# Two neighbouring attention groups in one run of score matmuls and one run of value matmuls

## The chip, the cores and the metric

The kernel runs on one core of a Trainium2 chip. The metric is the device time of one execution in microseconds (us); the median of three runs of the kernel before is 906.98 us (906.97 to 907.12). A core has a matrix engine (TensorE, PE in the profile, with its weight loads listed as PEld), a vector engine (DVE), a scalar engine (ACT) and a sync engine (SP) that issues the DMA transfers. Matmuls write into PSUM, which has eight banks of 2 KB in each of its 128 partitions; DVE and ACT read the banks.

## The reference

Three stages follow each other. Sparse attention over 4 batches, 8 heads, 576 positions and head width 64: in heads 0 to 3 a position looks back over the last 32 positions, in heads 4 to 7 over the earlier positions with the same remainder modulo 32. Then a two-layer MLP, then a gated MLP, both on 2304 tokens of width 512:

```
scores = q @ k^T / 8, masked;  attn = softmax(scores);  x = attn @ v        # 2304 x 512
x = leaky_relu(x @ moe_w_in, 0.01) @ moe_w_out                              # 512 -> 2048 -> 512
out = (sigmoid(x @ moe2_w_gate) * (x @ moe2_w_val)) @ moe2_w_out            # 512 -> 1536 -> 512
```

The weights arrive as 64-bit numbers; the kernel turns their bits into 32-bit words and splits each value into a high and a low part, so that each product is done as three fp32r matmuls (high by high, high by low, low by high; lines 329 to 331).

## The kernel before, in words

**Attention groups.** The 576 positions of each batch are halved: eight chunks `c` of 288 positions. A group is one chunk and one pair of heads (`pr`). Pairs 0 and 1 are local heads: five blocks of 64 queries by 96 keys. Pairs 2 and 3 are strided heads: five blocks of 63 queries by 63 keys in an even chunk; in an odd chunk the keys are 126, and the five blocks make two groups of three and two. That gives 40 groups in the order of `CORDER`, even chunks first. The first four groups have their own buffers.

**A group's work** (class `Group`): loads of q, k and v (lines 475 to 494); scores (line 509, tile `sc`, two matmuls a block, one for each head of 64 rows); masks by DVE (line 529, into `e`), row maxima (line 535), exponentials with their sums by ACT (line 540), the reciprocals and the scaling on DVE (lines 547 to 555); transposes of `e` on TensorE (line 564, tile `pt`), copied by ACT into `pts` (line 570); values (line 581, tile `xo`); and two parts of the result written as a high part by ACT (line 600) and a low part by DVE (line 598) into `x`. Scores use the four 64 by 64 quarters of the TensorE array, values its two column halves (or the quarters where there are 63 keys); transposes and MLP matmuls use the whole array.

**First MLP.** Class `First` takes one chunk of tokens and one slice of 128 hidden units: 12 matmuls from `x` into `h` (lines 329 to 331), ACT twice over `h` (lines 703 and 706), DVE once (line 710), and 12 matmuls from `gh`, `gl` into `y`. A run of 12 such matmuls of 256 columns is called an MLP run below. A token chunk can start when its groups have written `x`, so MLP runs of earlier chunks are laid between the attention work of later ones. Class `Job` prepares weights on ACT and DVE (lines 133 to 182).

**What sets the order.** All operations up to the end of the first MLP go into one list planner (class `Plan`). An operation has an engine, a cost in ns, operations that it comes after, a rank and rooms that it takes and gives. `Plan.order` places the operations by these costs, and the instructions of each engine then stand in that order and are executed in it. Rooms are buffers: `sc` is one pair of PSUM banks for scores (mm0, mm1; the `h` tiles use mm2 and mm3 during attention), `ax` two banks for transposes and values, `pts` two buffers, `e` and `st` three, `qk` three, `v` two. SP issues all loads from one queue in the planned order, so a load that waits for its buffer holds up the loads behind it.

**How banks are guarded.** In the built program an instruction waits for the last one that touched the tile it needs: a mask waits until the matmuls into its `sc` bank are done.

Of the kernel before, what the change touches and what calls it, by code (L numbers as in the profile page):

```python
# [7 lines left out]
F32 = mybir.dt.float32  # L8
# [8 lines left out]
P = 128  # L17
# [12 lines left out]
NB = 5  # L30
# [33 lines left out]
SPLIT = 2  # L64
OPS = 12
T0 = 256
GATES, OPERAND_PAIRS, LAG = 6, 8, 2

CONST_W = P + 2 * LW + SW[0] + SW[1]
# [3 lines left out]
def attention_mlp_glu(ctx: ExitStack, tc: tile.TileContext, qT, kl, ks0, ks1, vl, vs0, vs1, w1, w2, wg, wv, w3, const, out):  # L73
# [19 lines left out]
    def bank(tag, shape, name):  # L93
        return ps.tile(shape, F32, tag=tag, bufs=1, name=name)
# [191 lines left out]
    for c in range(NC2):  # L286
        quarter = {n: parts_tile(("p", c, n), [P, 2, 512]) for n in range(1, 8)}
        for m, w in enumerate((wg, wv)):
            d = {n: quarter[n][:, m, :] for n in quarter}
            a, b = Job((w, 2 * c)), Job((w, 2 * c + 1))  # L290
            a.whole = b.whole = False
            a.dest, b.dest, b.only = [d[1], d[2]], [None, d[3]], 1
            t = Sums(a, b, None, [d[5], d[6]])
# [15 lines left out]
    for i in range(len(cells) + 1):  # L309
        mine = [(i, "p", n) for n in ORDER] if i < len(cells) else []  # L310
# [24 lines left out]
    ap = att_pool.__enter__()  # L335
# [107 lines left out]
    class Group:  # L443


        def __init__(self, c, pr, blocks):
            self.c, self.pr, self.blocks, self.nb = c, pr, blocks, len(blocks)
            self.b, self.half = divmod(c, 2)
            self.local = pr < 2
            if self.local:  # L450
                self.w = LW
                self.q0 = [LOC[i] for i in blocks]
                self.k0 = [max(0, self.half * TA + LOC[i] - STRIDE) for i in blocks]
                self.nq = [LOC_N[i] for i in blocks]
                self.skip = [64 - n for n in self.nq]
            else:
                self.w = SW[self.half]
                self.q0 = [RES[i] * HP for i in blocks]
                self.k0 = [RES[i] * HP * (self.half + 1) for i in blocks]
                self.nq = [RES_N[i] * HP for i in blocks]  # L460
                self.skip = [SQ - n for n in self.nq]

            self.cut = (self.nb + 1) // 2

        def side(self, n, h):

            h = h if n < self.cut else 1 - h
            return slice(64 * h, 64 * h + 64)

        def buffers(self):  # L470
# [22 lines left out]
            src = vl[b, pr, self.half] if self.local else (vs0, vs1)[self.half][b, pr - 2]  # L493
            nc.sync.dma_start(out=self.v[:w, :nb, :], in_=src[:, self.blocks[0] : self.blocks[0] + nb, :])

        def scores(self, at):
            nb, w, cut = self.nb, self.w, self.cut
            sc = [
                bank(f"mm{j + 2 * ('h' in at)}", [P, z - a, w], f"sc{a}") for j, (a, z) in enumerate(((0, cut), (cut, nb)))
            ]  # L500
            for i in range(cut):
                for n in (i, cut + i):
                    if n >= (cut, nb)[n >= cut]:
                        continue
                    q0, k0 = self.q0[n] - self.q0[0], self.k0[n] - self.k0[0]
                    for h in range(2):
                        r = slice(64 * h, 64 * h + 64)
                        o = self.side(n, h)
                        nc.tensor.matmul(
                            sc[n >= cut][o, n - cut * (n >= cut), :], self.q[r, q0 : q0 + 64], self.k[r, k0 : k0 + w],  # L510
                            start=True, stop=True,
                        )
            self.sc = sc

        def parts(self):
            if self.local and self.half == 0:
# [42 lines left out]
        def tr(self, a, z, at):  # L559
            if a == 0:  # L560
                self.pt = {}
            self.pt[a] = bank(f"ax{at['ax'][0]}", [P, z - a, P], "pt")
            for n in range(a, z):
                nc.tensor.transpose(self.pt[a][: self.w, n - a, :], self.e[:, n, :], ident)

        def pts(self, a, z, at):
            w = self.w
            if a == 0:
                self.p = ap.tile([P, NB, P], F32, tag=f"pt{at['pts'][0]}", bufs=1, name="pts")
            nc.scalar.copy(self.p[:w, a:z, :], self.pt[a][:w, :, :])  # L570

        def pv(self, at):
# [26 lines left out]
            else:  # L599
                nc.scalar.copy(dst[0], src)  # L600

        def plan(self, n):

            nb, w, total = self.nb, self.w, sum(self.nq)
            rank = (1, n)
            self.buffers()
            qk, v = [] if self.c == 0 else ["qk"], [] if self.c == 0 else ["v"]
            me = self
            self.sc_room = ["h", "h"] if self.c == 0 and n % 2 else ["sc"]
            ax = ("ya", "yb")[n % 2] if self.c == 0 else "ax"  # L610
            lq = plan.add("SP", 4 * P * (self.q0[-1] + 64 - self.q0[0]), self.load_q, rank=(LOAD(n, 0),), me=me, take=qk)
            lk = plan.add(
                "SP", 4 * P * (self.k0[-1] + w - self.k0[0]), self.load_k, rank=(LOAD(n, 0) + 0.01,), me=me, then=[lq]
            )
            lv = plan.add("SP", 4 * w * nb * P, self.load_v, rank=(LOAD(n, 1),), me=me, take=v)
            sc = plan.add(
                "PE", 100 * nb, self.scores, rank=rank, me=me, kind="sc", after=[lq, lk], take=self.sc_room,
                give=qk,
            )
            before, parts = [sc, plan.const[0 if self.local else 2]], self.parts()  # L620
            for j, (a, z, _) in enumerate(parts):
                op = plan.add(
                    "DVE", (z - a) * w / 0.96 + 67, lambda at, j=j: self.mask(j, at), rank=(1, n, 0), me=me, after=before,
                    take=["e", "st"] if j == 0 else [], give=self.sc_room if j == len(parts) - 1 else [],
                )
                before = [op]
            op = plan.add("DVE", nb * w / 0.96 + 67, self.top, rank=(1, n, 1), me=me, after=before)
            op = plan.add("ACT", nb * (180 + w / 1.2 + 100 - 10), self.exps, rank=rank, me=me, after=[op])
            self.key = op
            op = plan.add("DVE", 75, self.eps, rank=(1, n, 2), me=me, after=[op])  # L630
            op = plan.add("DVE", 95, self.inverse, rank=(1, n, 3), me=me, after=[op])
            op = plan.add("DVE", nb * w / 0.96 + 67, self.norm, rank=(1, n, 4), me=me, after=[op], give=["st"])
            copies = []
            for a in range(0, nb, 3):
                z = min(a + 3, nb)
                t = plan.add(
                    "PE", 109 * (z - a), lambda at, a=a, z=z: self.tr(a, z, at), rank=rank, me=me, kind="pt", after=[op, plan.const[1]],
                    take=["ax"], give=["e"] if z == nb else [],
                )
                copies.append(  # L640
                    plan.add(
                        "ACT", (z - a) * P / 1.2 + 57, lambda at, a=a, z=z: self.pts(a, z, at), rank=rank, me=me, after=[t],
                        take=["pts"] if a == 0 else [], give=[("ax", t)],
                    )
                )
            pv = plan.add(
                "PE", 1.0 * total * 1.85, self.pv, rank=rank, me=me, kind="xo", after=copies + [lv], take=[ax],
                give=["pts"] + v,
            )
            self.done = []  # L650
            for s0, s1 in ((0, HP - 1), (HP - 1, HP)):
                m = total * (s1 - s0) // HP
                op = plan.add(
                    "ACT", m / 1.2 + 57, lambda at, s0=s0, s1=s1: self.put(s0, s1, False, at), rank=rank, me=me, after=[pv]
                )
                op = plan.add(
                    "DVE", m / 0.96 + 67, lambda at, s0=s0, s1=s1: self.put(s0, s1, True, at), rank=(1, n, 5), me=me,
                    after=[op], give=[(ax, pv)] if s0 else [],
                )
                self.done.append(op)  # L660

    groups = []
    for c in CORDER:
# [193 lines left out]
    total, last_read = {}, {}  # L857
# [275 lines left out]
    def load_const(a, z):  # L1133
        nc.sync.dma_start(out=cst[:, a:z], in_=const[:, a:z])

    plan = Plan(
        {
            "place": RING, "qk": 3, "v": 2, "e": 3, "st": 3, "sc": 1, "h": 2, "ax": 2, "ya": 1, "yb": 1, "pts": 2, "early": EARLY, "late": EARLY, "raw": STAGED, "w32": WORDS, "split": 1, "late split": SPLIT, "sums": 2,
        }
    )  # L1140
    unit_done, unit_place = {}, {}
    for j, (a, z) in enumerate(consts):
        op = plan.add("SP", 4 * P * (z - a), lambda at, a=a, z=z: load_const(a, z), rank=((0.5, 1.5, 2.5)[j],), me=plan)
        plan.const.append(op)
    for n, g in enumerate(groups):
        g.plan(n)

    def to_late(at):
        att_pool.__exit__(None, None, None)
# [14 lines left out]
    for j in range(RING, RING + n_a):  # L1164
        op = plan.add(
            "SP", 4096 * P, lambda at, j=j: fetch(j), rank=(-2000 + j,), after=[jobs[ready[uses[j]]].kept], then=before,
            take=["place"], me=plan,
# [14 lines left out]
    after = [op for item in final if item.t0 < 2 * TP for op in item.flushed]  # L1182
    after += [item.entered for item in final if item.t0 < XCUT] + [plan.add("-", 0, to_small, rank=(0,), me=plan, after=[item.left for item in items[:REGION]])]
    for n, name in enumerate(MAKE):
        steps = operand_steps(0, name)
        for engine, cost in enumerate((867, 735, 867)):
            if engine or name[0] == "s":
                op = plan.add(
                    ("DVE", "ACT", "DVE")[engine], cost, lambda at, steps=steps, engine=engine: steps(engine), rank=(1, n), me=plan,
                    after=after,  # L1190
# [122 lines left out]
```

## Time and profile before

| what | value |
|---|---|
| median of 3 runs | 906.98 us |
| the profiled execution, its own time | 909.16 us |
| its span, first to last instruction | 907.4 us |
| TensorE busy | 886.8 us (98%) |
| DVE busy | 714.3 us (79%) |
| ACT busy | 455.6 us (50%) |
| DMA | 214.49 MB, mean 236 GB/s |
| chain that ended last | TensorE 82% of the span |

The profiled execution took 1.8 us more than its span, for what lies before the first and behind the last instruction, and 2.2 us more than the median. Attention begins at once and its last value matmuls are done at 167.4 us; from then on TensorE has only whole-array matmuls. In the timeline each row is one instruction or several equal ones merged; an fp32 matmul of scores or values shows up as two rows' worth (x20 for the ten matmuls of a five-block group).

### The profile page before, as it was taken

Reading aid. Unit: us, or ns where it says so; the run is one execution under the profiler, and the core shown is the slowest. Engines: PE = TensorE matmul, PEld = TensorE weight load, DVE = VectorE, ACT = ScalarE, POOL = GpSimd, SP = SyncE. Lnnn points to the kernel's source line nnn. Section 1 sums busy time; section 2 is a strip of 40 time slices with the busy share of each in tenths; the row PEclk is TensorE's granted clock in tenths of the full one; section 3 lists DMA queues with packets and bytes.
Section 4 is the critical chain, followed back from the end, with each engine's and each line's share of the span. In section 5 each row is a group of like instructions: output and inputs, shape, how many; then the busy total and the mean of one; then the engine's idle time right before and its main releaser. Section 6 shows DMA issues by size and latency. Waiting matters only on the chain.

```text
span 907.4 us, 17636 instructions
## 1 busy us (share of the span) xinstructions
PE 886.8 (98%) x6399; PEld 831.5 (92%) x6399; DVE 714.3 (79%) x1570; ACT 455.6 (50%) x1196; POOL 0.2 (0%) x4
## 2 busy tenths in 40 slices
PE   6899999999999999999999999999999999999997
PEld 5788788998888999888899999999999999999997
DVE  6798899856888877787796767779967778667775
ACT  6688888544444444443553653335453344443331
POOL 0000000000000000000000000000000000000000
PEclk9889999999999999999999999999999999999999
DMA  8444846657676689664639877777887777887762
GB/s 247 146 149 128 264 123 213 215 224 295 233 264 222 215 285 408 221 244 164 216 137 321 319 240 251 256 251 258 257 311 254 252 246 266 293 280 246 243 233 70
DMA packets 81686, 214.49 MB, mean 236 GB/s; under 512 B 10216, under 2 KB 21832, under 8 KB 81600
## 3 DMA queue, kind: packets, MB, share of 16 engines
q1 hardware_dynamic: 81600, 213.37, 69.6%
q8 instruction: 51, 0.84, 0.4%
q14 instruction: 35, 0.29, 0.1%
HBM read 164.84 MB, written 48.50 MB: 235 GB/s over the span
## 4 chain that ended last, share of the span: by engine, by line
PE 82%; DMA 6%; DVE 5%; ACT 3%; issue 1%; SPq 1%; ACTq 0%; DVEq 0%
PE h L329 6%; PE h L330 6%; PE h L331 6%; PE y L329 5%; PE y L330 5%; PE y L331 5%; PE g L879 5%; PE g L880 5%; PE v L881 5%; PE v L880 5%; PE v L879 5%; PE g L881 5%; PE o L935 5%; PE o L934 5%; PE o L933 5%; DMA raw<-w 3%
## 5 line engine op out<-in xcount | busy, mean ns | idle before, releaser
L948 DVE TENSOR_TENSOR sum_o<-o,sum_o 128x512 f32<-128x512 f32 x214 | 110.4, 549 | 34.9 <-PE o L935 34.8
L329 PE MATMUL h<-x,u 128*128 128x256 f32 (+2 forms) x384 | 132.6, 345 | 0.0
L329 PE MATMUL y<-gh,u 128*128 128x256 f32 (+2 forms) x384 | 131.3, 342 | 0.6 <-ACT sum_y L738 0.5
L330 PE MATMUL h<-x,u 128*128 128x256 f32 (+2 forms) x384 | 130.3, 339 | 0.0
L331 PE MATMUL h<-x,u 128*128 128x256 f32 (+2 forms) x384 | 130.2, 339 | 0.0
L330 PE MATMUL y<-gl,u 128*128 128x256 f32 (+2 forms) x384 | 129.4, 337 | 0.1
L331 PE MATMUL y<-gh,u 128*128 128x256 f32 (+2 forms) x384 | 129.3, 337 | 0.0
L935 PE MATMUL o<-u,gl 128*128 128x256 f32 x357 | 100.6, 282 | 0.0
L934 PE MATMUL o<-u,gh 128*128 128x256 f32 x357 | 100.4, 281 | 0.0
L933 PE MATMUL o<-u,gh 128*128 128x256 f32 x357 | 100.1, 280 | 0.0
L914 ACT CAST gh<-gate 128x384 fp32r<-128x384 f32 x123 | 63.2, 514 | 70.2 <-DVE gate L904 42.4
L879 PE MATMUL g<-ops,u 128*128 128x384 f32 x252 | 84.8, 336 | 0.0
L880 PE MATMUL g<-ops,u 128*128 128x384 f32 x252 | 84.5, 335 | 0.0
L881 PE MATMUL g<-ops,u 128*128 128x384 f32 x252 | 84.4, 335 | 0.0
L879 PE MATMUL v<-ops,u 128*128 128x384 f32 x252 | 84.2, 334 | 0.0
L880 PE MATMUL v<-ops,u 128*128 128x384 f32 x252 | 84.2, 334 | 0.0
L881 PE MATMUL v<-ops,u 128*128 128x384 f32 x252 | 84.2, 334 | 0.0
L329 PEld LDWEIGHTS h<-x,u 128*128 128x128 f32 x384 | 74.0, 193 | 8.0 <-issue 1.9
L703 ACT ACTIVATE gh<-h 128x256 fp32r<-128x256 f32 (+2 forms) x96 | 46.8, 488 | 67.3 <-PE y L331 61.0
L329 PEld LDWEIGHTS y<-gh,u 128*128 128x128 f32 x384 | 72.9, 190 | 7.5 <-issue 0.9
L330 PEld LDWEIGHTS h<-x,u 128*128 128x128 f32 x384 | 74.1, 193 | 5.7
L331 PEld LDWEIGHTS h<-x,u 128*128 128x128 f32 x384 | 74.0, 193 | 5.6
(83 smaller groups left out, 1908.5 us busy)
## 6 DMA issues: line engine op xcount, KB each, us to landing
u<-parts SPq DMA_DIRECT2D x203, 512.0 KB
parts<-split SPq DMA_DIRECT2D x127, 256.0 KB
raw<-w SPq DMA_DIRECT2D x44, 512.0 KB
parts<-split SPq DMA_DIRECT2D x20, 512.0 KB
raw<-wg SPq DMA_DIRECT2D x12, 512.0 KB
raw<-wv SPq DMA_DIRECT2D x12, 512.0 KB
out<-sum_o SPq DMA_DIRECT2D x16, 256.0 KB
u<-parts SPq DMA_DIRECT2D x15, 256.0 KB
```

Source lines behind the costliest of these rows:

```text
L329: nc.tensor.matmul(o, wu[:, 0, a:b], xh, start=start, stop=False)
L330: nc.tensor.matmul(o, wu[:, 0, a:b], xl, start=False, stop=False)
L331: nc.tensor.matmul(o, wu[:, 1, a:b], xh, start=False, stop=stop)
L703: nc.scalar.activation(out=self.g[0], in_=self.h, func=AF.Prelu, alpha=SLOPE)
L879: nc.tensor.matmul(o, wh, xh, start=first and k == 0, stop=False, **more)
L880: nc.tensor.matmul(o, wh, xl, start=False, stop=False, **more)
L881: nc.tensor.matmul(o, wl, xh, start=False, stop=k == 1, **more)
L914: nc.scalar.copy(self.part[name][0], self.tile[0, n])
L933: nc.tensor.matmul(o, gh, u[:, 0:256], start=first and r % 2 == 0, stop=False, **more)
L934: nc.tensor.matmul(o, gh, u[:, 256:512], start=False, stop=False, **more)
L935: nc.tensor.matmul(o, gl, u[:, 0:256], start=False, stop=True, **more)
L948: nc.vector.tensor_tensor(out=acc, in0=o, in1=acc, op=ALU.add)
```

## The change

From the fifth group on, groups are planned two at a time: 18 pairs of neighbours, which always have the same chunk and the same key width. `pair_scores` lays the scores of both into the same two banks, the second group's halves crosswise (`turned`), and issues both groups' matmuls one after the other; both groups' masks must be done before the banks are free again. `pair_pv` issues the values of both groups in one run; it takes both `ax` banks. A group's two sets of transposes now follow each other on TensorE (`then=self.turns`), and the `pts` buffer is taken by the transposes, not by the copy behind them. A pair's two `v` buffers come free together behind the pair's values, and its two `qk` buffers behind the pair's scores. The order of all engines changes, since the planner places everything anew.

```diff
+PAIRED = 4
...
+            self.cut, self.turned = (self.nb + 1) // 2, False
...
+            h = h if (n < self.cut) != self.turned else 1 - h
...
+        def pair_scores(self, other, at):
+
+            a, b, c, d = self.cut, self.nb - self.cut, other.nb - other.cut, other.cut
+            both = [bank(f"mm{j}", [P, n, self.w], f"sc{j}") for j, n in enumerate((a + c, b + d))]
+            self.sc = [both[0][:, :a, :], both[1][:, :b, :]]
+            other.sc = [both[1][:, b:, :], both[0][:, a:, :]]
+            other.turned = True
+            for g in (self, other):
+                g.scores(at, both)
+
+        def pair_pv(self, other, at):
+            for n, g in enumerate((self, other)):
+                g.pv({"ax": at["ax"][n:]})
...
                 t = plan.add(
                     "PE", 109 * (z - a), lambda at, a=a, z=z: self.tr(a, z, at), rank=rank, me=me, kind="pt", after=[op, plan.const[1]],
-                    take=["ax"], give=["e"] if z == nb else [],
+                    then=self.turns, take=["ax"] + (["pts"] if a == 0 else []),
+                    give=["e"] if z == nb else [],
                 )
+                self.turns = [t]
...
+    def plan_groups(n, mine):
+
+        for i, g in enumerate(mine):
+            g.plan_loads(n + i)
+        first, single = mine[0], len(mine) == 1
+        sc_room = ["h", "h"] if first.c == 0 and n % 2 else ["sc"]
+        ax = ("ya", "yb")[n % 2] if first.c == 0 else "ax"
+        sc = plan.add(
+            "PE", sum(100 * g.nb for g in mine), first.scores if single else lambda at: first.pair_scores(mine[1], at),
+            rank=(1, n), me=first, kind="sc", after=[op for g in mine for op in g.loads[:2]], take=sc_room,
+        )
+        for g in mine:
+            plan.free([sc], g, *g.held[0])
+            g.plan_softmax(sc)
+        plan.free([g.masked for g in mine], first, *sc_room)
+        pv = plan.add(
+            "PE", sum(1.85 * sum(g.nq) for g in mine), first.pv if single else lambda at: first.pair_pv(mine[1], at),
+            rank=(1, n), me=first, kind="xo", after=[op for g in mine for op in g.copies + g.loads[2:]], take=[ax] * len(mine),
+        )
...
-    for n, g in enumerate(groups):
-        g.plan(n)
+    n = 0
+    while n < len(groups):
+        mine = groups[n : n + (2 if n >= PAIRED else 1)]
+        plan_groups(n, mine)
+        n += len(mine)
```

TensorE in the steady part, before: the scores of the 15th group (`sc_1124`, line 509) and the values of the 11th (line 581), between transposes (`pt`) and MLP runs (`h`, `y`).

```order
L331 MATMUL h<-x_61,u_996 128x256
L564 MATMUL pt<-cst,e 63x128 x2
L564 MATMUL pt<-cst,e 96x128 x3
L509 MATMUL sc_1124<-k,q 64x63 x2
L509 MATMUL sc_1125<-k,q 64x63 x2
...
L581 MATMUL xo<-pts,v 64x63 x8
L581 MATMUL xo<-pts,v 64x36 x2
L564 MATMUL pt<-cst,e 96x128 x2
L329 MATMUL y<-gh,u_632 128x256
```

TensorE at the corresponding place in the changed kernel: the scores of the 13th and 14th group in the banks `sc_899` and `sc_900` (line 513), directly followed by the values of the 9th and 10th group (line 597).

```order
L332 MATMUL h<-x_61,u_358 128x256
L582 MATMUL pt<-cst,e 96x128 x5
L513 MATMUL sc_899<-k,q 64x96 x2
L513 MATMUL sc_900<-k,q 64x96 x2
...
L597 MATMUL xo<-pts,v 64x64 x8
L597 MATMUL xo<-pts,v 64x32 x2
...
L330 MATMUL h<-x_61,u_425 128x256
```

In the first, one group's scores and one group's values stand between transposes that use the whole array, and a group's transposes stand in two pieces; in the second, two groups' scores and two groups' values follow each other, and the five transposes of a group are together.

ACT behind the first MLP runs, before: `gh` and `g` are the two passes over `h`, line 540 the exponentials of the fifth and then the sixth group, line 177 a step of the weights.

```order
L703 ACTIVATE gh<-h 128x256
L706 ACTIVATE g<-h 128x256
L540 ACTIVATE e,st<-e,st 128x96 x5
L703 ACTIVATE gh<-h 128x256
L177 CAST u_518<-w 128x512
L706 ACTIVATE g<-h 128x256
L540 ACTIVATE e,st<-e,st 128x96 x5
```

ACT at the same place in the changed kernel (line 557 the exponentials, 745 and 748 the passes over `h`).

```order
L745 ACTIVATE gh<-h 128x256
L748 ACTIVATE g<-h 128x256
L178 CAST u_474<-w 128x512
L745 ACTIVATE gh<-h 128x256
L748 ACTIVATE g<-h 128x256
L557 ACTIVATE e,st<-e,st 128x96 x10
```

The exponentials of the fifth group have moved behind the passes over the second `h`, and those of the sixth follow at once.

## Rows read from the trace of the kernel before

**Rows 1.** Busy time by stretch: bounds, length, each engine's busy us, clock, DMA, GB/s.

```profile
20.00:54.24 34.24, 29.02 (x357) 24.74 (x355) 28.52 (x88) 25.49 (x108) 0.00 (x0) 0.82 0.59 177
54.24:167.42 113.18, 110.63 (x1476) 97.84 (x1475) 101.99 (x330) 93.62 (x390) 0.00 (x0) 1.00 0.56 174
110.00:140.00 30.00, 29.91 (x400) 26.24 (x400) 29.47 (x100) 25.16 (x105) 0.00 (x0) 1.00 0.51 156
167.42:907.40 739.98, 734.55 (x4423) 699.50 (x4419) 571.60 (x1118) 323.24 (x643) 0.00 (x0) 1.00 0.72 248
```

**Rows 2.** Timeline of TensorE around 110 us: start, duration, line, tiles, count.

```profile
109.02 0.28 PE L331 MATMUL h<-x,u 128*128 128x256 f32 x1
109.23 0.78 PE L581 MATMUL xo<-pts,v 96*64 96x64 f32 x20
109.93 0.53 PE L564 MATMUL pt<-cst,e 128*96 128x128 f32 x3
110.39 0.65 PE L509 MATMUL sc<-k,q 64*64 64x126 f32 x12
110.97 0.39 PE L329 MATMUL y<-gh,u 128*128 128x256 f32 x1
111.19 0.28 PE L330 MATMUL y<-gl,u 128*128 128x256 f32 x1
111.31 0.28 PE L331 MATMUL y<-gh,u 128*128 128x256 f32 x1
...
112.51 0.71 PE L564 MATMUL pt<-cst,e 128*96 128x128 f32 x5
112.97 0.36 PE L329 MATMUL h<-x,u 128*128 128x256 f32 x1
```

**Rows 3.** The same view, where two groups' values already follow each other.

```profile
114.58 1.15 PE L581 MATMUL xo<-pts,v 96*64 96x64 f32 x32
115.66 0.45 PE L509 MATMUL sc<-k,q 64*64 64x126 f32 x8
```

**Rows 4.** Timeline of TensorE: the first MLP run, and the first of the second chunk.

```profile
22.10 1.20 PE L509 MATMUL sc<-k,q 64*64 64x96 f32 x18
23.23 0.58 PE L329 MATMUL h<-x,u 128*128 128x256 f32 x1
...
51.53 0.56 PE L329 MATMUL h<-x,u 128*128 128x256 f32 x1
...
52.53 0.41 PE L330 MATMUL h<-x,u 128*128 128x256 f32 x1
52.75 0.41 PE L331 MATMUL h<-x,u 128*128 128x256 f32 x1
```

**Rows 5.** What TensorE waited for, 54.24 to 167.42: us, times, longest.

```profile
PE xo L581 <- DMA v<-vs: 1.6, 2, 0.9
```

**Rows 6.** Timeline of SP and TensorE: issue of a v load, and the values behind it.

```profile
91.37 0.36 SPq L494 DMA_DIRECT2D v<-vs  x1
...
97.61 0.43 PE L581 MATMUL xo<-pts,v 126*64 126x63 f32 x8 [0.86 <-DMA v<-vs]
```

**Rows 7.** Busy time by stretch again, for the clock in the early part.

```profile
28.00:31.40 3.40, 1.86 (x44) 1.29 (x42) 2.28 (x9) 1.72 (x8) 0.00 (x0) 0.99 0.32 87
31.40:38.20 6.80, 5.83 (x44) 5.16 (x44) 4.41 (x12) 4.88 (x24) 0.00 (x0) 0.50 0.38 120
48.40:55.30 6.90, 6.40 (x54) 5.36 (x56) 6.33 (x20) 5.78 (x28) 0.00 (x0) 0.51 0.58 182
```

**Rows 8.** Timeline of ACT: the first of the fifth group's exponentials.

```profile
26.74 0.38 ACT L540 ACTIVATE e<-e,st 128x96 f32<-128x96 f32 x1
```

**Rows 9.** Timeline: a group's scores on TensorE, and its first mask on DVE.

```profile
28.36 0.71 PE L509 MATMUL sc<-k,q 64*64 64x96 f32 x20
...
29.12 0.26 DVE L529 SCALAR_TENSOR_TENSOR e<-sc,cst 128x96 f32<-128x96 f32 x1 [1.21 <-PE sc L509]
```

More of the change, by code (lines that the diff above doesn't have):

```diff
@@ L461, in __init__ @@
                 self.skip = [SQ - n for n in self.nq]
-            self.cut = (self.nb + 1) // 2
+            self.cut, self.turned = (self.nb + 1) // 2, False
         def side(self, n, h):
-            h = h if n < self.cut else 1 - h
+            h = h if (n < self.cut) != self.turned else 1 - h
             return slice(64 * h, 64 * h + 64)
@@ L494, in load_v, with scores @@
             nc.sync.dma_start(out=self.v[:w, :nb, :], in_=src[:, self.blocks[0] : self.blocks[0] + nb, :])
-        def scores(self, at):
+        def scores(self, at, both=None):
             nb, w, cut = self.nb, self.w, self.cut
-            sc = [
-                bank(f"mm{j + 2 * ('h' in at)}", [P, z - a, w], f"sc{a}") for j, (a, z) in enumerate(((0, cut), (cut, nb)))
-            ]
+            if both is None:
+                both = [
+                    bank(f"mm{j + 2 * ('h' in at)}", [P, n, w], f"sc{j}")
+                    for j, n in enumerate((cut, nb - cut))
+                ]
+                self.sc = both
             for i in range(cut):
@@ L509, in scores @@
                         nc.tensor.matmul(
-                            sc[n >= cut][o, n - cut * (n >= cut), :], self.q[r, q0 : q0 + 64], self.k[r, k0 : k0 + w],
-                            start=True, stop=True,
-                        )
-            self.sc = sc
+                            self.sc[n >= cut][o, n - cut * (n >= cut), :], self.q[r, q0 : q0 + 64],
+                            self.k[r, k0 : k0 + w], start=True, stop=True,
+                        )
+        def pair_scores(self, other, at):
[9 more added lines that the diff above has]
+                g.pv({"ax": at["ax"][n:]})
         def parts(self):
@@ L561, in tr @@
                 self.pt = {}
+                self.p = ap.tile([P, NB, P], F32, tag=f"pt{at['pts'][0]}", bufs=1, name="pts")
             self.pt[a] = bank(f"ax{at['ax'][0]}", [P, z - a, P], "pt")
@@ L567, in pts @@
             w = self.w
-            if a == 0:
-                self.p = ap.tile([P, NB, P], F32, tag=f"pt{at['pts'][0]}", bufs=1, name="pts")
             nc.scalar.copy(self.p[:w, a:z, :], self.pt[a][:w, :, :])
@@ L600, in put, with plan_loads @@
                 nc.scalar.copy(dst[0], src)
-        def plan(self, n):
-            nb, w, total = self.nb, self.w, sum(self.nq)
-            rank = (1, n)
+        def plan_loads(self, n):
+            nb, w, me = self.nb, self.w, self
+            self.n, self.rank = n, (1, n)
             self.buffers()
             qk, v = [] if self.c == 0 else ["qk"], [] if self.c == 0 else ["v"]
-            me = self
-            self.sc_room = ["h", "h"] if self.c == 0 and n % 2 else ["sc"]
-            ax = ("ya", "yb")[n % 2] if self.c == 0 else "ax"
             lq = plan.add("SP", 4 * P * (self.q0[-1] + 64 - self.q0[0]), self.load_q, rank=(LOAD(n, 0),), me=me, take=qk)
@@ L615, in plan, with plan_softmax @@
             lv = plan.add("SP", 4 * w * nb * P, self.load_v, rank=(LOAD(n, 1),), me=me, take=v)
[L616 to L619, printed above, removed]
+            self.loads, self.held = [lq, lk, lv], (qk, v)
+        def plan_softmax(self, sc):
+            nb, w, me, n, rank = self.nb, self.w, self, self.n, self.rank
             before, parts = [sc, plan.const[0 if self.local else 2]], self.parts()
@@ L623, in plan @@
                     "DVE", (z - a) * w / 0.96 + 67, lambda at, j=j: self.mask(j, at), rank=(1, n, 0), me=me, after=before,
-                    take=["e", "st"] if j == 0 else [], give=self.sc_room if j == len(parts) - 1 else [],
+                    take=["e", "st"] if j == 0 else [],
                 )
                 before = [op]
+            self.masked = op
             op = plan.add("DVE", nb * w / 0.96 + 67, self.top, rank=(1, n, 1), me=me, after=before)
@@ L632, in plan @@
             op = plan.add("DVE", nb * w / 0.96 + 67, self.norm, rank=(1, n, 4), me=me, after=[op], give=["st"])
-            copies = []
+            self.copies, self.turns = [], []
             for a in range(0, nb, 3):
@@ L637, in plan, with plan_puts @@
                     "PE", 109 * (z - a), lambda at, a=a, z=z: self.tr(a, z, at), rank=rank, me=me, kind="pt", after=[op, plan.const[1]],
-                    take=["ax"], give=["e"] if z == nb else [],
-                )
-                copies.append(
+                    then=self.turns, take=["ax"] + (["pts"] if a == 0 else []),
+                    give=["e"] if z == nb else [],
+                )
+                self.turns = [t]
+                self.copies.append(
                     plan.add(
                         "ACT", (z - a) * P / 1.2 + 57, lambda at, a=a, z=z: self.pts(a, z, at), rank=rank, me=me, after=[t],
-                        take=["pts"] if a == 0 else [], give=[("ax", t)],
+                        give=[("ax", t)],
                     )
                 )
[L646 to L649, printed above, removed]
+        def plan_puts(self, pv, ax, then):
+            total = sum(self.nq)
             self.done = []
@@ L653, in plan @@
                 op = plan.add(
-                    "ACT", m / 1.2 + 57, lambda at, s0=s0, s1=s1: self.put(s0, s1, False, at), rank=rank, me=me, after=[pv]
+                    "ACT", m / 1.2 + 57, lambda at, s0=s0, s1=s1: self.put(s0, s1, False, at), rank=self.rank, me=self, after=[pv]
                 )
                 op = plan.add(
-                    "DVE", m / 0.96 + 67, lambda at, s0=s0, s1=s1: self.put(s0, s1, True, at), rank=(1, n, 5), me=me,
-                    after=[op], give=[(ax, pv)] if s0 else [],
+                    "DVE", m / 0.96 + 67, lambda at, s0=s0, s1=s1: self.put(s0, s1, True, at), rank=(1, self.n, 5), me=self,
+                    after=[op], then=then, give=[(ax, pv)] if s0 else [],
                 )
                 self.done.append(op)
+    def plan_groups(n, mine):
[16 more added lines that the diff above has]
+        )
+        then = []
+        for g in mine:
+            plan.free([pv], g, "pts", *g.held[1])
+            g.plan_puts(pv, ax, then)
+            then = [g.done[1]]
     groups = []
```

## The prediction

> **What bounds the kernel now.** I read busy time by stretch first. Behind the last value matmul, at 167.42 us, TensorE is busy 734.55 of 739.98 us; nothing of that part is touched, so what the change is worth is decided before it. From 54.24 to 167.42, where MLP runs fill the attention, TensorE is busy 110.63 of 113.18 us, DVE 101.99 and ACT 93.62 [rows 1]. TensorE sets the end there too. From 20 to 54.24 it is busy 29.02 of 34.24, at a granted clock of 0.82: that head waits for softmax chains.
>
> The timeline around 110 us shows that busy is not the same as at work. Two MLP matmuls follow each other after 0.12 us (111.19 to 111.31), but from the last one of a run to the first value matmul it is 0.21 (109.02 to 109.23) [rows 2]: entering the divided array costs 0.09. Leaving shows where two groups' values already share a run: 32 instructions take 1.08 us (114.58 to 115.66) [rows 3]. The first 20 of them alone take 0.70 (109.23 to 109.93) [rows 2]; the other 12 would add some 0.50 alone, at the same 0.035 each and a tail, 1.20 in all. So one exit is worth 0.12. From transposes the entry is dearer: five transposes up to an MLP matmul take 0.46 us (112.51 to 112.97), three up to scores also 0.46 (109.93 to 110.39) [rows 2]; two transposes at 0.09 vanish in the turn, 0.18. Entry is thus 0.09 to 0.18 and exit 0.12; I take 0.24 for a visit to the divided array, with 0.21 and 0.30 as ends. The first step of an MLP run is long as well, 0.22 (110.97 to 111.19), but such runs are entered 40 times in the old order and in the new one, so that stays.
>
> **The change part by part.** The instructions are the same in number on every engine; only their order changes. Both orders have done the same attention work when the first MLP run of the second token chunk begins (51.53 us before) [rows 4]: scores and values of eight and four paired groups, transposes of five, four MLP runs. I cut there.
>
> *Behind the cut.* Counted in the two orders from that run to the last value matmul, stretches of scores and values between whole-array work fall from 42 to 18: scores 13 to 16 and values 9 to 12 now follow each other, and no transposes split them. 24 fewer visits at 0.24 are 5.8 us less (5.0 to 7.2). TensorE is the bound here, so they count in full unless another engine takes over (below). Changes from scores to values inside a visit stay about as many, 15 and 12, and are left at nothing.
>
> *Transposes.* A group's five now stand together; this is in the count. They cost the fill between them: before, MLP runs or scores lay between the two pieces and covered ACT's copies. Now an MLP run lies behind them, so a cover stays; what it lacks is in the next term.
>
> *Values of a pair take both `ax` banks.* They can't start until ACT has copied the second group's transposes, and the next pair's transposes can't start until ACT and DVE have written out this pair's values. The orders keep one MLP run in front of each pair of values and scores plus one or two runs behind, so most of it is covered. Placing the first pairs behind the cut by the rows' durations I find waits of 0.45, 0.2 and 0 us. For 14 pairs I take 0.15 each, 2.1 us; nothing and 0.45 each (6.3) are the ends. Queued behind a waiting value run are the MLP runs, and behind them ACT's passes over `h`.
>
> *Loads.* Both `v` of a pair are issued only behind the pair before. Today TensorE waits 1.6 us for `v`, twice [rows 5]; the later of these loads was issued at 91.37 and its values ran at 97.61, 6.2 us on [rows 6]. At the same place of the new order three MLP runs (4.5 us by 12 times 0.12), a pair's scores (1.1) and five transposes (0.5) lie between a pair's values and the next, 6.1 us: the wait nearly goes, but a second load now stands behind the first. I take half, 0.8 us less; 1.6 less and 1.6 more are the ends. On SP the loads of q and k stand between those `v`; a pair's second q and k are issued when the scores before are done, one pair's time ahead (113.18 us for 14 pairs, 8 us), against 6.2 for the load above: nothing.
>
> *The head.* Here a walk decides, since TensorE waits. The first MLP run loses the scores that stood in front of it and begins at 22.2 instead of 23.23 [rows 4], ending at 24.8 by 12 times 0.21. The pair's scores follow at half clock, 2.1 us by twice the 1.13 of the fifth group's last part less an exit [rows 4], to 27.0; the second MLP run, at full clock from 28 [rows 7], ends at 28.9. ACT's order puts both passes over that second `h` ahead of the exponentials, so the fifth group's begin at some 30 instead of 26.74 [rows 8], 3 us later, and the sixth's follow at once. The seventh and eighth, whose scores now come early together, catch up. Following norm, transposes, copies and values from there, the pair of groups 11 and 12 gets its scores at 45, when DVE has masked groups 9 and 10, and the second chunk's run begins at 51.3. The rows at half clock step by 0.21 (52.53 to 52.75) [rows 4]; half clock before lasts from 48.4 to 55.3 [rows 7] and by the walk should end about 52, so the run ends at 53.0 against 54.24: 1.2 us less. Ends: all 5.2 us of idle time there gone, or a further 6.8 us at half clock in full work, 3.4 us more.
>
> In that walk a pair's masks start when the whole run of scores is done. The row: a group's scores take 0.71 us from 28.36 and its first mask starts at 29.12, 0.05 behind them [rows 9]. The Trainium skill (PSUM — Partial Sum Buffer, section "Summary: rules for kernel authors") says to guard PSUM by the bank and quadrant, not by the address; for two groups in one bank that makes the first one's masks wait for the second one's matmuls, some 0.6 us. By that reading the head gains the 1.2 us above; if groups were guarded by their own columns, it would gain about 1.8.
>
> *The sum.* 5.8 + 1.2 + 0.8 less, 2.1 more: 5.7 us less. The profiled execution took 909.16 us, 907.4 of it span; it would come to 903.5. The median of the runs shown, 906.98, lies 2.2 under the profiled one, so the forecast is 901.3, and its own range, by the ends of the visits and half of what the waits leave open, is 899.5 to 903.5.
>
> **The rivals.**
>
> *DVE becomes the bound.* From 110 to 140 DVE is busy 29.47 of 30 us, TensorE 29.91 [rows 1]. A TensorE that needs less time there would wait for masks and low parts. For: it is 98% busy over some 50 us of the 113, so 10 or 11 of the 24 visits, 2.5 us, could come back as waiting. Against: the new order lays eight more MLP runs in front of the last values, which spreads DVE's attention work over more TensorE time. Time: 903.8.
>
> *The chain through `ax` decides.* If each of 14 pairs waits 0.5 us, as the worst of the three I placed, that is 7.0 instead of 2.1: 906.2, no change. For: ACT executes in order, and a group's five exponentials (1.9 us at 0.38 [rows 8]) can stand in front of a copy. Against: the MLP runs between.
>
> *Half clock, the slower side.* TensorE's clock fell to 1.2 GHz (0.50 and 0.51) in two stretches of 6.8 us, each behind idle time: 1.54 us of the 3.4 before the first [rows 7]. The walk has TensorE idle 2.7 us before groups 11 and 12's scores, and again before the next transposes. If half clock then lasts two such stretches into the part where TensorE is the bound, each costs 3.4 us, and the head's 1.2 us go with them, since its last run falls into the first: 901.3 + 8.0 = 909.3. One stretch alone, the head's gain kept, gives 904.7; from two on the kernel is slower. The Trainium skill (TensorE: Matmul & The Clock Gate, section "HAM oscillation — how this bites in real kernels") describes this: idle gaps throw the array back to half clock and the next work starts cold. The rows agree for the head; behind 54.24 the clock is 1.00 through a wait of 0.86 [rows 1, 6].
>
> *The head's idle time goes altogether.* 5.2 instead of 1.2, and no half clock: 897.3.
>
> **How the numbers follow.** The forecast has 0.55, DVE as the bound 0.18, the `ax` chain 0.12, half clock 0.08, the free head 0.07. A measurement of this kernel can tell 0.2%, 1.8 us, from no change, so faster means under 905.2 and slower over 908.8. The forecast's cases are nearly all faster (0.53 of 0.55), of DVE's 0.15, of the chain's 0.03, all of the free head's: 0.78. Slower are most of half clock's and a little of the chain's, 0.09; the rest, 0.13, is no change. The range reaches from near the free head to near the chain: 897.5 to 906.0.
>
> **What would show it.** Right: stretches of scores and values on TensorE between MLP runs fall to about half in number, each as long as two; the gaps around one stay at 0.2 us; from the second chunk's first run to the last values TensorE spends some 6 us less on the same work, and that run ends near 53 us. Wrong: value runs with waits on ACT's `pts` or transposes with waits on DVE's `x` at most pairs (the chain); waits on DVE's `e` between 110 and 160 (DVE); matmul steps of 0.21 us after 56 us (the clock); or a pair's run that takes as long as its two groups apart, which would take the 5.8 away.

## The result, and the profile after

The changed kernel takes 894.8 us (894.04 to 895.55) against 906.98; the ratio is 0.9875, with a 95% interval of 0.9858 to 0.9892, so 10 to 13 us less. The forecast was 901.3, its range 897.5 to 906.0: the direction is right, the gain twice what was forecast, and the time lies 2.7 us under the range. In later series of 15 to 25 runs the kernel before has medians of 905.2 to 906.0; on the chip of run e8 below the gain is 10.8 us (905.2 to 894.4).

Busy time by stretch, changed kernel: bounds and length, each engine's busy us (instructions), granted clock of TensorE, DMA share, GB/s. The first row ends where the first MLP run of the second chunk ends (the cut), the second with the last value matmul.

```profile
20.00:51.50 31.50, 25.32 (x362) 22.40 (x359) 29.32 (x89) 25.82 (x110) 0.00 (x0) 0.85 0.62 190
51.50:166.12 114.62, 113.75 (x1573) 107.79 (x1572) 107.54 (x345) 95.81 (x400) 0.00 (x0) 1.00 0.60 185
166.12:893.10 726.98, 722.25 (x4327) 688.04 (x4323) 565.09 (x1105) 319.09 (x632) 0.00 (x0) 1.00 0.73 251
110.00:140.00 30.00, 29.74 (x435) 28.02 (x439) 29.41 (x98) 25.51 (x106) 0.00 (x0) 1.00 0.68 209
42.20:52.40 10.20, 9.31 (x107) 8.72 (x107) 9.04 (x29) 8.56 (x35) 0.00 (x0) 0.50 0.71 226
```

The clock column counts the part before the first recorded change of the clock as 1.00, but the matmuls there step by 0.21 us, which is half clock: up to 27.87 us in the first profile of before, up to 24.95 here. So the 0.82 of [rows 1] and the 0.85 here are too high. The stretches at half clock named below are those of the record, behind this start.

The second and third row are read together with the same two of before [rows 1], since eight MLP runs have moved from one to the other. TensorE's own time from the cut on is 113.75 + 722.25 = 836.00 us against 110.63 + 734.55 = 845.18: 9.2 less. Its idle time there is 0.87 + 4.73 against 2.55 + 5.43: 2.4 less. The run at the cut ends at 51.50 instead of 54.24: 2.7 less. That adds up to the 14.3 us between the two profiled spans (907.4 and 893.1). Since the median moved by 12.2 only, the kernel before was profiled once more, together with a further profile of the changed one (runs e9 and e8 below):

| term, us | forecast | first two profiles | e9 to e8 |
|---|---|---|---|
| end of the head | -1.2 | -2.7 | -1.65 |
| TensorE's waits behind it | +1.3 | -2.4 | -2.3 |
| TensorE's own time behind it | -5.8 | -9.2 | -8.4 |
| sum | -5.7 | -14.3 | -12.3 |

Both pairs of profiles lie further apart than the medians (12.2 and 10.8 us), so the terms are somewhat too large in sum.

Timeline of TensorE, changed kernel: one pair's scores directly followed by another pair's values, between MLP runs.

```profile
68.27 0.28 PE L332 MATMUL h<-x,u 128*128 128x256 f32 x1
68.48 1.06 PE L513 MATMUL sc<-k,q 64*64 64x96 f32 x40
69.47 1.36 PE L597 MATMUL xo<-pts,v 96*64 96x64 f32 x40
70.75 0.39 PE L330 MATMUL y<-gh,u 128*128 128x256 f32 x1
```

And TensorE before, one group's scores between transposes and an MLP run.

```profile
75.26 0.54 PE L564 MATMUL pt<-cst,e 128*63 128x128 f32 x3
75.73 0.71 PE L509 MATMUL sc<-k,q 64*64 64x96 f32 x20
76.37 0.39 PE L329 MATMUL h<-x,u 128*128 128x256 f32 x1
```

One local group's scores hold TensorE from 75.73 to 76.37, 0.64 us; a pair's from 68.48 to 69.47, 0.99, where twice 0.64 is 1.28. So the pair saves 0.29 in the scores alone, before any entry is counted. A pair's values, 1.28 (69.47 to 70.75), save 0.12 against twice the 0.70 of [rows 2]. The entry from transposes (75.26 to 75.73, three transposes, 0.47) costs 0.17 more than three transposes before an MLP run (0.30 where values stand ahead of them), the entry from an MLP run 0.09.

The first group's masks wait for the whole run of scores, as the prediction's walk had it: DVE is free for 1.54 us, the pair's scores end at 79.80, and the first mask starts at 79.85, behind all of them. TensorE and DVE, changed kernel:

```profile
78.96 0.84 PE L513 MATMUL sc<-k,q 64*64 64x126 f32 x18
79.85 0.42 DVE L546 SCALAR_TENSOR_TENSOR e<-sc,cst 128x252 f32<-128x252 f32 x1 [1.54 <-PE sc L513]
```

What TensorE waited for from the cut to the last values, changed kernel: us, times, longest.

```profile
PE xo L597 <- DMA v<-vs: 0.5, 2, 0.3
PE pt L582 <- DVE x L614: 0.3, 1, 0.3
```

The waits for `v` are down from 1.6 [rows 5] to 0.5, and the pairs' waits for `pts` or `x` that I charged with 2.1 are one wait of 0.3. In e8 the same list has none for `v`, but 0.7 for `pts`, 0.3 for `x` and 0.2 for `st`, one wait each. DVE is busy 29.41 of 30 us between 110 and 140, as before, but TensorE waits there for 0.26 us in all.

### The profile page after: what moved, and what is told of

The parts are those of the page before. It is cut to its first block, busy times and chain, and to the rows that moved or that the text cites. A ratio compares the mean times of both kernels' runs of the same rounds, so it can differ in the third digit from the quotient of the medians.

```text
span 893.1 us, 17642 instructions
## 1 busy us (share of the span) xinstructions
PE 873.8 (98%) x6399; PEld 827.5 (93%) x6399; DVE 714.1 (80%) x1570; ACT 453.9 (51%) x1196; POOL 0.2 (0%) x4
## 4 chain that ended last, share of the span: by engine, by line
PE 92%; DMA 3%; ACT 2%; DVE 1%; SPq 1%; issue 0%; DVEq 0%
PE h L330 7%; PE y L330 7%; PE h L331 7%; PE h L332 7%; PE y L331 7%; PE y L332 7%; PE g L921 5%; PE g L922 5%; PE v L922 5%; PE v L923 5%; PE v L921 5%; PE g L923 5%; PE o L977 5%; PE o L976 5%; PE o L975 5%; PE xo L597 2%
```

## The experiments

Theory A: a visit to the divided array costs 0.38 us, not 0.24. Theory B: the 0.24 holds, and waits that the new rules for transposes and buffers removed make up the rest. Theory C: the head and its clock. Theory D, formed before e5: the price depends on how a visit begins and ends.

**e1, no pairs.** `-PAIRED = 4` `+PAIRED = 40`

> The changed kernel with no pair at all (PAIRED = 40): only the new rule that a group's transposes follow each other and that the transposes take the pts buffer is left. Behind the first run of the second token chunk TensorE enters the divided array 41 times instead of 42 in the kernel before and 18 in the changed one. Theory A (each such visit costs 0.38 us, which is what the two traces give: 9.2 us over 24 visits): 907 minus 0.4, so 905 to 908.5, as before. Theory B (a visit costs the 0.24 us of the forecast and the rest of the gain is waiting removed by the new transposes and buffer rules): 904.5 or less.

Measured: 905.6 against 906.0 us, ratio 0.9997 (0.9978 to 1.0017). The adjacent transposes and the `pts` rule by themselves give nothing that can be measured; the gain needs the pairs. B's form of the missing waits falls.

**e2, pairs from the 13th group on.** `-PAIRED = 4` `+PAIRED = 12`

> Pairs only from the 13th group on (PAIRED = 12), so that the head up to 50 us is planned with single groups as in the kernel before. 22 visits behind the cut. Theory A (0.38 us a visit, the head's 2.7 us apart from it): 20 visits fewer, 7.6 us less: 899.4, between the two kernels. Theory B (0.24 a visit): 4.8 less, 902.2. Theory C (most of the gain is the head and its clock): within 2 us of the kernel before.

Measured: 895.85, ratio 0.9890 (0.9867 to 0.9914), some 10 us less. With 14 of the 18 pairs nearly all of the gain is there, so C falls. TensorE's own time from the cut on is 111.64 + 725.12 = 836.76 us (first rows of the next fence), 7.7 less than e9's 844.49, or 0.39 for each of 20 visits. The rest is waiting again: 0.82 us idle up to the last values instead of 2.78.

**e3, only the scores in pairs; e4, only the values.** The edit of e3; e4 does the same with the scores; `...` stands for what is left out.

```
-        pv = plan.add("PE", sum(1.85 * ...), first.pv if single else lambda at: first.pair_pv(...), ..., take=[ax] * len(mine))
         for g in mine:
+            pv = plan.add("PE", 1.85 * sum(g.nq), g.pv, rank=g.rank, me=g, kind="xo", after=g.copies + g.loads[2:], take=[ax])
             plan.free([pv], g, "pts", *g.held[1])
...
```

> Scores in pairs, values of each group by themselves. 34 visits behind the cut. Theory A: 8 fewer than before at 0.38, 3.0 us less: 904.0. Theory B: 8 at 0.24, 1.9 less: 905.1. If the two groups' scores gain by themselves, because the second group's matmuls fill the quarters that the first leaves free at its end (0.29 us in 0.99 against twice 0.64), 14 pairs give some 3 us whatever the number of visits, and it comes out at 902 or less.

> Values in pairs, scores of each group by themselves. 31 visits behind the cut. Theory A: 11 fewer than before at 0.38, 4.2 us less: 902.8. Theory B: 11 at 0.24, 2.6 less: 904.3. If pairing the values brings waits through both ax banks, 2.1 us come on top and it is about as slow as before.

Measured: e3 899.85 (0.9931, 0.9908 to 0.9955), e4 899.0 (0.9928, 0.9905 to 0.9950). Both beat A and B; e3 is what its third case had (902 or less). Busy time of e2, e3 and e4 in turn, each up to its last values and behind them:

```profile
51.77:164.23 112.46, 111.64 (x1548) 104.80 (x1548) 105.81 (x340) 94.82 (x400) 0.00 (x0) 1.00 0.62 192
164.23:894.10 729.87, 725.12 (x4351) 690.92 (x4347) 566.11 (x1107) 320.01 (x635) 0.00 (x0) 1.00 0.72 249
```

```profile
52.45:161.95 109.50, 108.82 (x1489) 100.09 (x1488) 100.55 (x329) 92.77 (x390) 0.00 (x0) 1.00 0.58 180
161.95:896.30 734.35, 729.44 (x4387) 695.24 (x4383) 570.17 (x1116) 322.77 (x641) 0.00 (x0) 1.00 0.73 250
```

```profile
51.08:173.90 122.82, 122.40 (x1596) 112.07 (x1596) 114.12 (x356) 100.22 (x409) 0.00 (x0) 1.00 0.61 190
173.90:898.00 724.10, 719.38 (x4303) 685.13 (x4299) 559.49 (x1094) 316.32 (x626) 0.00 (x0) 1.00 0.73 249
```

With the scores paired TensorE's own time is 838.26, 6.2 less than 844.49; but one group's values and three transposes are done before the cut here, about 1.0 us by their steps of 0.70 and 0.3, so 5.2 less, for 8 visits fewer. With the values paired it is 841.78, 2.7 less for 11 visits. So one price for every visit does not fit: it would be 0.65 in e3 and 0.25 in e4. The count hides two things. In e3 14 pairs of scores are joined, 0.37 for each, whatever the number of visits; and the entries from transposes, 19 before, are 7 in e3 and 10 in e4. Waits up to the last values are 0.68 and 0.42 us.

**e5, e6, e7: the price of a visit by itself.** One whole-array matmul more per pair between its scores (e5), between its values (e6), or one in front of each paired group's transposes (e7, where no visit is added); e8 is the changed kernel beside them.

```
+ nc.tensor.matmul(both[0][:, a, :63], ident, ident[:, :63], start=True, stop=True)      # e5, before the second group's scores
+ nc.tensor.matmul(self.xo[:, :63], ident, ident[:, :63], start=True, stop=True)         # e6, before the second group's values
+ nc.tensor.matmul(self.pt[a][:, 0, :63], ident, ident[:, :63], start=True, stop=True)   # e7, before the group's transposes
```

> The changed kernel with one whole-array matmul (128x63, fp32, its result is overwritten) put between the two groups' scores of each pair: the order of all else stays, and each pair's score run is cut into two visits, 18 in all, 14 of them behind the cut. Measured against e7, which has such matmuls where the array is whole anyway. Theory A (0.38 us a visit whatever it holds): 14 times 0.38, 5.3 us above the changed kernel plus 1 to 2 for the matmuls themselves. Theory D (a visit's price depends on what it ends with: a pair's scores take 0.99 against twice 0.64, and an entry from a matmul like the transposes costs 0.17 more): 14 times 0.46, 6.4 plus 1 to 2. Theory B (0.24): 3.4 plus 1 to 2.

> The same matmul put between the two groups' values of each pair instead: 18 visits more, 16 behind the cut. Theory A: 16 times 0.38, 6.1 us plus 1 to 2. Theory D (a pair's values take 1.29 against twice 0.70, so only 0.11 in the exit, and 0.17 at the entry): 16 times 0.28, 4.5 plus 1 to 2, less than e5 although it has more visits behind the cut. Theory B: 3.8 plus 1 to 2.

> The control: the same matmul in front of each paired group's transposes, where TensorE works with the whole array anyway, 36 in all, no visit more. By the transposes' 0.108 us for 128 columns a matmul of 63 columns in fp32 costs 0.05 to 0.2 us: 2 to 6 us above the changed kernel, half of which is the part to be taken off from e5 and from e6.

> The changed kernel as it is, on the chip of e5 to e7, so that these are compared with it there: 894 to 896.

Measured: e5 903.0, e6 901.2, e7 900.5, e8 894.4 us (ratios to before 0.9977, 0.9958, 0.9941 and 0.9879, each with an interval of 0.0017 to 0.0034 to either side). e7's 36 matmuls cost 6.1 us, so 18 cost 3.05, and e5 has 5.6, e6 3.8 us on top of that. The timelines show the price at one place. TensorE in e5, e6 and e7:

```profile
70.19 0.71 PE L513 MATMUL sc<-k,q 64*64 64x96 f32 x20
70.84 0.43 PE L527 MATMUL sc<-cst 128*128 128x63 f32 x2
71.20 0.71 PE L513 MATMUL sc<-k,q 64*64 64x96 f32 x20
71.84 0.34 PE L601 MATMUL xo<-pts,v 96*64 96x64 f32 x4
```

```profile
69.25 0.78 PE L599 MATMUL xo<-pts,v 96*64 96x64 f32 x20
69.96 0.43 PE L593 MATMUL xo<-cst 128*128 128x63 f32 x2
70.32 0.78 PE L599 MATMUL xo<-pts,v 96*64 96x64 f32 x20
71.03 0.39 PE L330 MATMUL y<-gh,u 128*128 128x256 f32 x1
```

```profile
67.06 0.33 PE L582 MATMUL pt<-cst 128*128 128x63 f32 x2
67.23 0.71 PE L584 MATMUL pt<-cst,e 128*96 128x128 f32 x5
67.69 0.36 PE L330 MATMUL h<-x,u 128*128 128x256 f32 x1
```

Beside transposes the matmul takes 0.17 us (67.06 to 67.23). Between scores it makes 0.99 into 1.65 (70.19 to 71.84), 0.66 more, so a visit with entry and exit costs 0.49 here; between values 1.28 becomes 1.78 (69.25 to 71.03), 0.50 more, 0.33 a visit.

The difference of 0.16 between the two is, by the rows, no price of a visit. A group of five blocks has no work for two of the four quarters at its end: its last four matmul rows start two in 0.08 us, where a pair's start four in 0.08 us to the end, so a joint run saves two such steps, 0.16 us. The eight odd-chunk pairs (three and two blocks) have no such saving, since one half-filled block ends the run either way. Their scores, joined in the changed kernel and cut in e5:

```profile
111.20 0.86 PE L513 MATMUL sc<-k,q 64*64 64x126 f32 x20
111.99 0.39 PE L330 MATMUL y<-gh,u 128*128 128x256 f32 x1
```

```profile
115.25 0.65 PE L513 MATMUL sc<-k,q 64*64 64x126 f32 x12
115.83 0.43 PE L527 MATMUL sc<-cst 128*128 128x63 f32 x2
116.19 0.45 PE L513 MATMUL sc<-k,q 64*64 64x126 f32 x8
116.57 0.38 PE L330 MATMUL y<-gh,u 128*128 128x256 f32 x1
```

Here 0.79 becomes 1.32, 0.53 more, 0.36 a visit: nearly that of values. So a visit costs 0.33 to 0.36 in both kinds of work, entered from a matmul like this one, and the scores of two five-block groups gain 0.16 beside it.

Over all pairs behind the cut, TensorE's own time up to the last values in e5, e6 and e7:

```profile
52.40:173.57 121.17, 121.17 (x1601) 112.85 (x1600) 108.72 (x345) 96.63 (x401) 0.00 (x0) 1.00 0.57 175
```

```profile
51.26:171.75 120.49, 120.49 (x1606) 113.26 (x1604) 109.44 (x345) 97.13 (x403) 0.00 (x0) 1.00 0.58 176
```

```profile
51.74:170.92 119.18, 118.66 (x1635) 113.25 (x1634) 108.77 (x344) 97.06 (x401) 0.00 (x0) 1.00 0.58 178
```

Against 113.75 that is 7.4 for 14 cuts, 6.7 for 16 and 4.9 for 31 matmuls: 0.53, 0.42 and 0.16 each, so on average 0.37 for a cut in scores and 0.26 for one in values (less than at the places above; why was not taken apart). e5 alone would fit A (0.38) as well; e6 does not. The order is D's, with smaller sizes than it gave (0.46 and 0.28), and the larger price of scores lies in part in the quarters. Put back together, 14 times 0.37 and 16 times 0.26 are 9.3 us, about as much as the 8.4 to 9.2 of TensorE's own time that the change saved. The Trainium skill (TensorEngine Tiling (Array Packing), section "Key Properties") says that changing the tiling mode drains TensorE, without a price; the runs agree in so far as each change costs time, and give these prices.

**e9, the kernel before once more.** No edit.

> The kernel before, one more profile: if its head (start of the second token chunk's first run, its end at 54.2 in the first profile) and the 1.5 us of stalls in the later first MLP are the same, they are the kernel's own and belong to the gain; if the run ends at 50 to 52 or the stalls are gone, the profiled execution was a long one and some 2 of the 14.3 us between the two profiles are no gain of the change.

```profile
20.00:51.81 31.81, 25.67 (x369) 22.05 (x368) 28.78 (x90) 25.82 (x110) 0.00 (x0) 0.95 0.64 189
48.40:51.81 3.41, 3.08 (x31) 2.88 (x23) 3.41 (x13) 3.17 (x15) 0.00 (x0) 0.56 0.65 175
51.81:164.81 113.00, 110.22 (x1478) 97.62 (x1476) 102.60 (x332) 93.56 (x390) 0.00 (x0) 1.00 0.57 174
164.81:904.80 739.99, 734.27 (x4422) 699.57 (x4419) 571.13 (x1117) 322.76 (x643) 0.00 (x0) 1.00 0.72 248
```

The same for e8, the changed kernel again:

```profile
50.16:165.33 115.17, 113.69 (x1573) 107.55 (x1571) 107.43 (x344) 95.72 (x401) 0.00 (x0) 1.00 0.60 184
165.33:892.50 727.17, 722.42 (x4327) 688.06 (x4323) 564.04 (x1105) 318.85 (x632) 0.00 (x0) 1.00 0.73 251
```

e9 took 906.55 us. Its head ends at 51.81, 2.4 us earlier than in the first profile, though TensorE is idle longer there (6.14 us of the stretch against 5.22): the recorded clock is 0.95 instead of 0.82. Behind the start, where the matmuls step by 0.21 up to 27.46 here, half clock comes once, from about 48.4 on, where the first profile had it from 31.4 to 38.2 as well and up to 55.3 [rows 7]. So much of the first pair's 2.7 us was the clock of one execution. From the cut on e9 repeats the first profile: 844.49 us of TensorE's own time (845.18) and 8.50 us of idle time (7.98).

**e10 to e12, other plans with pairs.** `+PAIRED = 8`; then in the planner, where TensorE may prefer rank to an earlier start within so many ns, `-NEAR = {"PE": 150` `+NEAR = {"PE": 500` and `60`.

> Pairs from the ninth group on (PAIRED = 8): the groups whose chain TensorE waits for in the head are single again. 20 visits behind the cut instead of 18: 0.7 us more at 0.35. If pairs in the head cost idle time there, the head is 1 us shorter and it comes out equal to the changed kernel, 894 to 895.5; if the head's time is DVE's work (93% busy there), pairs or not, 895 to 896.

> A candidate: the changed kernel with a planner that prefers rank over an earlier start within 500 ns on TensorE instead of 150. 16 visits behind the cut instead of 18, six of them entered from transposes instead of two, and ten entered from MLP runs instead of 16; attention ends nine MLP runs earlier in the order. By the prices of the rows: two visits less 0.7, four more entries from transposes at 0.09 more each, 0.4: 894.1, no change that can be measured. If the fuller order makes DVE or ACT late, waits add 1 to 4 us.

> The other way, 60 ns: 16 visits, but nine entered from transposes and seven followed by transposes: two visits less 0.7, seven more entries from transposes 0.6, six more transposes behind a visit at 0.05, 0.3: 894.6, as the changed kernel.

Measured: 899.1 (0.9935, 0.9914 to 0.9955), 905.1 (0.9987, 0.9970 to 1.0004) and 926.1 (1.0229, 1.0205 to 1.0253). None beats the changed kernel, and all three expectations missed. What TensorE waited for up to the last values in e10, then in e11, then the first rows in e12:

```profile
PE pt L582 <- DVE x L614: 1.2, 2, 0.8
PE pt L582 <- ACT gh L745: 0.6, 1, 0.6
PE pt L582 <- DVE e L572: 0.5, 1, 0.5
```

```profile
PE xo L597 <- DMA v<-vs: 2.7, 2, 2.0
PE sc L513 <- DMA k<-ks: 1.0, 1, 1.0
PE pt L582 <- DVE st L564: 1.0, 2, 0.7
PE pt L582 <- DVE x L614: 1.0, 3, 0.4
PE pt L582 <- DVE e L572: 0.2, 1, 0.2
```

```profile
PE pt L582 <- DVE x L614: 5.9, 5, 2.6
PE xo L597 <- DMA v<-vs: 4.1, 3, 1.9
```

In e10 waits are the smaller part: over the whole profile TensorE is idle 1.8 us longer than in the changed kernel and busy 3.0 us more, which no run takes apart. e11 has two visits fewer than the changed kernel behind the cut and is 10 us slower: 6.15 us idle instead of 0.87, a head that ends at 53.94, and 3.4 us of half clock behind it. In e12 TensorE is idle for 18.3 us, and its clock falls in the middle of the attention as well, in three stretches of 10 us like this one and a shorter one:

```profile
110.20:120.50 10.30, 8.68 (x66) 7.29 (x66) 8.52 (x30) 8.74 (x38) 0.00 (x0) 0.50 0.98 306
```

These are the chain through `ax` (waits for `x`), the late loads and the half clock that the prediction weighed. The changed kernel's order avoids most of them. Whether an order without pairs would pay them at these two settings was not run.

## Why the direction was right and the size wrong

*Visits: the mechanism right, the size too small.* One step that failed is "I take 0.24 for a visit to the divided array, with 0.21 and 0.30 as ends". The count, 24 fewer, was right; the term came to 8.4 to 9.2 us instead of 5.8, 0.35 to 0.38 a visit. Three things were missing in the 0.24. Of the entries that went, 17 of 24 were from transposes (19 became 2), at 0.17, where 0.24 leaves 0.12 for an entry. The first transpose behind a visit is slower too (three take 0.30 us there and 0.24 behind an MLP run), and 21 of 22 such exits went. And in the scores of the six five-block pairs behind the cut the second group fills the quarters that the first leaves idle, 0.16 a pair; the prediction had nothing for that. The exit of 0.12, read from values [rows 2, 3], is about right for scores too: of the 0.29 that a pair saves, 0.13 remain. An estimate from these rows is 17 times 0.29, 7 times 0.21, 21 times 0.06 and 6 times 0.16: 8.6 us, inside what was measured. The runs show that joining pairs gives the gain (e1, e2) and what a cut costs (e5 to e7); how it divides among these three is worked out from rows, not from runs of their own.

*The waits: wrong in sign, and the larger miss.* The other step that failed is "For 14 pairs I take 0.15 each, 2.1 us": with 0.8 less for `v` that made 1.3 more in all. Measured, the waits behind the cut are 2.3 to 2.4 us fewer, 3.6 to 3.7 off, where the visits were 2.6 to 3.4 off. Waits for `pts` and `x` up to the last values are 0.3 us in the first profile of the changed kernel and 1.0 in e8, for all pairs together. In most places the MLP runs in front of a pair's values cover the copies; the 0.45 of the walk was not typical. The `v` waits shrink from 1.6 and 1.3 to 0.5 and none. 0.7 to 1.0 us of the idle time that went lies in the later first MLP, where both profiles of before wait for sums of `y`; the changed kernel doesn't, nor does e1, which has no pairs. Why the old plan is late there was not tried.

*The head: size near, by luck.* 1.2 less was forecast for the run at the cut, 1.65 and 2.7 were measured, but two executions of the kernel before differ by 2.4 there, and the way was another. The walk let that run begin at 51.3 against 51.53 and win the rest by an earlier return to full clock. It began at 48.79 and, in e8, at 47.66. In the first of these it stayed at half clock to its end and took 2.71 us, just as in the first profile of before. The half clock reached over the end of the head, for 10.2 us in the first profile after (42.20 to 52.40), and ended 0.9 us behind the cut, not two stretches into the full work. Nor did idle time go: from the start to the cut TensorE is idle 13.65 and 14.00 us in the changed kernel and 12.59 and 14.27 in the kernel before. It is busy 3.8 and 1.4 us less; how much of that is the clock is not shown.

*The rivals.* DVE is as busy as was feared between 110 and 140 and yet not waited for; that the eight MLP runs that moved in front of the last values kept TensorE supplied, as the "against" had it, fits this, but no run takes them away. The chain and the half clock did not decide here. In e12 both cost time; in e11 late loads cost most of the listed waits.

## What to carry to other kernels

Price a change of array mode from runs of its kind in the trace, the entry and the exit each by what stands on the other side: here 0.33 to 0.36 us for one more visit entered from a short whole-array matmul, with entries from transposes dearer than from long matmuls. Joining small tiled matmuls can pay more than the transitions, where one group fills the part of the array that the other leaves idle at its end; count that by itself. But a plan with fewer visits is only worth having if its waits stay covered: in e11 two visits fewer came with 5 us more waiting behind the cut.

## What the runs showed of the hardware beside that

Two executions of the kernel before had recorded clocks of 0.82 and 0.95 between 20 us and the cut; behind the start, which ran at half clock in both, one had two stretches at 1.2 GHz and one had one. The execution with less of it had more idle time there (6.14 against 5.22 us); the end of that part moved by 2.4 us. In this kernel, whose head waits, two single profiles can differ by this much with no change at all.
